# Loading Exp's table behind head 0's two copies, copying head 0's key on ScalarE, and giving the ninth pair of unit 6 the tanh formula

## The chip, the cores and the metric

The kernel runs on one core of a Trainium2 chip. The metric is the device time of one execution in microseconds (us); what is compared is the median of several executions. The core has five engines, each with its own instruction stream: PE (TensorE, matrix products; PEld is its loading of weights), DVE (VectorE), ACT (ScalarE), POOL (GpSimd) and SP (SyncE, which here only issues DMAs). An engine works through its stream in order and waits for the others through semaphores.

## The reference

Two layers follow each other: attention whose mask comes from nearest centroids, and a gated feed-forward layer behind an RMS norm.

```python
def _attn_ref(q, k, v, centroids):            # q, k, v: 4 x 8 x 768 x 64; centroids: 8 x 16 x 64
    scale = 1.0 / np.sqrt(D)
    q_n, k_n, c_n = (a / (norm(a) + 1e-06) for a in (q, k, centroids))
    q_assign = np.argmax(np.einsum('bhsd,hcd->bhsc', q_n, c_n), axis=-1)
    k_assign = np.argmax(np.einsum('bhsd,hcd->bhsc', k_n, c_n), axis=-1)
    mask = q_assign[:, :, :, None] == k_assign[:, :, None, :]
    scores = np.where(mask, scale * (q @ k.T), -1000000000.0)
    attn = softmax(scores)
    return attn @ v

def _moe_ref(x, w_gate, w_val, w_out, rms_g): # x: 3072 x 512, w_gate and w_val: 512 x 1536
    xn = x / np.sqrt(np.mean(x * x) + 1e-06) * rms_g
    g = xn @ w_gate
    silu = g * (1.0 / (1.0 + np.exp(-g)))
    return silu * (xn @ w_val) @ w_out
```

## The kernel before

The 4 batches of 768 tokens are cut into 8 units of 384 tokens (`UNITS`, numbered 0 to 7). For each unit the kernel computes the attention of 8 heads, and while the heads of unit u run, the feed-forward work of unit u-1 and the output products of unit u-2 are woven between them. The 32 pairs of batch and head are in 8 groups of 4. The mask is folded into the score product: the key and query tiles (`kext`, `qext`) hold 64 rows of numbers and 16 rows that say which centroid is nearest, so that one product with 80 rows gives masked scores.

The program order is written out by hand; each engine gets its instructions in that order.

The start is what the first two edits touch. ACT takes the square root for the centroids' norm (L182, `c_norm`), which needs one table of functions, and then an Exp on one column (L184, `first_exp`), whose result nobody reads: it makes the table for Exp come early. Each change of table appears as an ACT_TABLE_LOAD in ACT's stream. DVE scales the centroids (L187, L188), PE transposes them (L192), DVE copies them into `cblk` (L193, L194). For a head, `trans` transposes its key or query on PE into a PSUM tile (L221) and copies it to `qkT` (L225 on DVE, or L227 on ACT by a Copy). The PSUM tiles for this come from one pool of three buffers (`ps_g`), so that a fourth transpose waits until the first has been copied. POOL casts `qkT` to bf16 rows of `kext` and `qext` (L240): K0 and K1 are the two halves of a key, Q0 and Q1 of a query, each an instruction of 64 x 384.

Which centroid is nearest comes from `pair_clusters`: PE multiplies `qkT` with `cblk` (L320), DVE transposes the product (L323), takes the largest of each 16 (L326) and compares (L327, both inputs in SBUF, into a bf16 tile `pads`). `head` puts the result under the key and the query (L332). The hand-written order of POOL's casts at the start is: K0, Q0, K1 of head 0; K0, Q0, K1 of head 1; K0, K1, Q0 of head 2 and of head 3; Q1 of heads 0 and 1; then the cast of head 0's values (`vcast`, L243), the DMAs of the first quarter of the gate and value weights (L204), and the values of head 1. The product of the first probabilities with the values (`pv`, L366) needs head 0's values. On PE it stands ahead of the cluster products of heads 4 and 5, which the second half of DVE's chain at the start works on. Unit 0's attention is followed by its norm (L391, L402, the steps L144 to L153, L410), the transposes to `xnT` (L425) and the first gate products (L442).

The end is what the third edit touches. A feed-forward unit has 12 pairs (FC = 12): a gate product and a value product, four matmuls each (L442), into buffers of `ps_g`. With `CUT = 16`, pairs 0 to 7 of a unit are woven into the attention, and pairs 8 to 11 come behind it; `rest` is what is left of unit 6, the seventh. SiLU is computed in two ways. Where Exp's table stays loaded, it is a Tanh on ACT (L450), and DVE adds 1 and multiplies by the gate product in PSUM (L451), then multiplies by half the value product (L455). Where `last` holds, no Exp follows: ACT takes Silu (L448), which needs another table, and DVE multiplies once with the value product (L453). The first item of `rest` is pair 8's gate; behind it stands the last head's product with the values (`pv`, whose result DVE scales in L371 and L373), then pair 8's value and the other pairs. After pair 9 come the last squares of unit 7's norm (L393) and its root (`root`), then unit 6's output products (L467), unit 7's 12 pairs, and its output products (L467, L478).

Of the kernel before, what the change touches and what calls it, by code (L numbers as in the profile page):

```python
# [14 lines left out]
ACT = mybir.ActivationFunctionType  # L15
# [7 lines left out]
def kernel(  # L23
# [12 lines left out]
    nc = tc.nc  # L36
# [11 lines left out]
    NU = len(UNITS)  # L48
# [5 lines left out]
    CUT = 2 * FC - 8  # L54
# [117 lines left out]
    off = const.tile([P, 1], F32)  # L172
# [8 lines left out]
    c_norm = const.tile([P, 1], F32)  # L181
    nc.scalar.activation(c_norm, c_ss, ACT.Sqrt)  # L182
    first_exp = const.tile([P, 1], F32)
    nc.scalar.activation(first_exp, off, ACT.Exp)  # L184
    c_inv = const.tile([P, 1], F32)
    nc.vector.reciprocal(c_inv, c_norm)
    nc.vector.tensor_scalar_mul(c_n[:, :D], c_in, c_inv)  # L187
# [2 lines left out]
    def centroids_t():  # L190
        c_ps = ps_s.tile([P, P], F32, tag="s", name="c_ps")
        nc.tensor.transpose(c_ps, c_n, ident_f)  # L192
        nc.vector.tensor_copy(cblk[:D, :, :NC], c_ps[:D].rearrange("d (h c) -> d h c", c=NC))  # L193
        nc.vector.tensor_copy(cblk[D:, :, NC:], c_ps[D:].rearrange("d (h c) -> d h c", c=NC))  # L194
# [17 lines left out]
    def trans(g, h, part, on=None):  # L212
        if (g, h // 2) not in qkT:
            qkT[g, h // 2] = qk32.tile([P, 2, 2, UQ], F32, tag="qkT", name="qkT")
        qk = staged[g * HG + h]
        if g * HG + h >= BH:
            nc.vector.transpose(qkT[g, h // 2][:, h % 2, part], qk[:, part].rearrange("p t d -> p (t d)"))
            return
        ps = ps_g.tile([P, UQ], F32, tag="gen", name="tq")
        for i in range(HT):  # L220
            nc.tensor.transpose(ps[:, i * P:(i + 1) * P], qk[:, part, 2 * i:2 * i + 2].rearrange("p t d -> p (t d)"),  # L221
                                ident_f)
        to, by = qkT[g, h // 2][:, h % 2, part], 1.0 / ZS if part and g < BG else 1.0
        if on is nc.vector:
            nc.vector.tensor_scalar_mul(to, ps, by)  # L225
        else:
            nc.scalar.activation(to, ps, ACT.Copy, scale=by)  # L227
# [84 lines left out]
    def pair_clusters(p, heads=(0, 1)):  # L312
        g, h = divmod(2 * p, HG)
        what = [(h + i, m) for i in heads for m in range(2)]
        at = [slot(2 * p + i, m) for i in heads for m in range(2)]
        r = slice(min(at), max(at) + 32)
        pool = ps_g if p else ps_s
        ps = pool.tile([P, UQ], F32, tag="gen" if p else "s", name="sc")
        for a, (hh, m) in sorted(zip(at, what)):
            nc.tensor.matmul(ps[a:a + 32], lhsT=cblk[:, g * HG + hh], rhs=qkT[g, hh // 2][:, hh % 2, m],  # L320
                             start=True, stop=True)
        sct = asg.tile([P, UQ], F32, tag="scT", name="scT", bufs=2)
        nc.vector.transpose(sct[r], ps[r])  # L323
        cl = sct[r].rearrange("p (b e c) -> p b e c", e=2, c=NC)
        mx = small.tile([P, NB, 2], F32, tag="mx", name="mx")[r]
        nc.vector.tensor_reduce(mx, cl, axis=AX, op=ALU.max)  # L326
        nc.vector.tensor_tensor(pads[p][r, :, :NC].rearrange("p b c e -> p b e c"), cl,  # L327
                                mx.unsqueeze(3).broadcast_to([mx.shape[0], NB, 2, NC]), op=ALU.is_equal)
# [105 lines left out]
    def gv(u, f, val):  # L434
        if f == 0 and not val:
            gvT[u] = xp.tile([P, FC, UQ], BF16, tag="gvT", name="gvT")
        w = wv if val else wg
        n = UNITS[u][2] * P
        full = ps_g.tile([P, UQ], F32, tag="gen", name="val" if val else "gate")
        ps = full[:, :n]  # L440
        for c in range(CC):
            nc.tensor.matmul(ps, lhsT=w[:, c, f * P:(f + 1) * P], rhs=xnT[u][:, c, :n], start=c == 0, stop=c == CC - 1)  # L442
        last = u == NU - 1 or (u, f >= CUT // 2) == (NU - 2, True)
        if not val:
            th = gate.tile([P, UQ], F32, tag="th", name="th")[:, :n]
            gates[u] = th
            if last:
                nc.scalar.activation(th, ps, ACT.Silu)  # L448
            else:
                nc.scalar.activation(th, ps, ACT.Tanh, scale=0.5)  # L450
                nc.vector.scalar_tensor_tensor(th, th, 1.0, ps, op0=ALU.add, op1=ALU.mult)  # L451
        elif last:
            nc.vector.tensor_mul(gvT[u][:, f, :n], gates[u], ps)  # L453
        else:
            nc.vector.scalar_tensor_tensor(gvT[u][:, f, :n], gates[u], 0.5, ps, op0=ALU.mult, op1=ALU.mult)  # L455
# [89 lines left out]
    def ffn_work(u):  # L545
        n = UNITS[u][2] / HT
        return [(0.64 * n, lambda f=f, val=val: gv(u, f, val)) for f in range(FC) for val in (False, True)]
# [15 lines left out]

    K0, K1, Q0, Q1 = (1, 0), (1, 1), (0, 0), (0, 1)
    pool_ = nc.gpsimd
    trans(0, 0, 1, nc.vector)
    centroids_t()
    trans(0, 0, 0)
    trans(0, 1, 1)
    pair_clusters(0, (0,))  # L570
    casts(pool_, 0, K0, Q0, K1)
# [173 lines left out]
```

## Time and profile before

| | |
|---|---|
| Device time, median of 4 runs | 327.99 us (327.66 to 328.29) |
| Device time of the profiled execution | 327.66 us |
| Its span, from the first to the last instruction | 325.9 us |
| Instructions | 7780 |
| Granted TensorE clock in the profiled execution | 1.00 |
| DMA traffic | 34.63 MB, mean 106 GB/s |

The span is the part of the device time in which the program's instructions run; 1.8 us lie around it. All times in what follows count from the span's start. In a line of the timeline the columns are: start and length in us, engine, line of the program, operation, tile written and tiles read, size, count, and in brackets the idle time before it and what ended it. Lines with the same group may be merged into one with a count. The end of a matmul is modelled. A line of the windows holds, behind the stretch and its length, the busy time and the number of instructions of each engine, the granted clock, the share of the DMA engines and their rate.

### The profile page before, as it was taken

What the parts mean: (1) busy time and instruction counts of PE and PEld (TensorE: products, weight loads), DVE (VectorE), ACT (ScalarE), POOL (GpSimd) and SP (SyncE); (2) the same over time, 40 slices, a digit from 0 to 9 for tenths busy, and PEclk for the clock granted to TensorE, in tenths of its full rate; (3) what the DMA queues carried; (4) which work ended last, traced back from release to release, by engine and by line L of the source; (5) the groups of instructions that cost most, each with busy time, mean ns of one, the idle gap of its engine ahead of it and who ended that gap; (6) DMA issues with size and microseconds to landing.
All of it is one profiled execution on the core that took longest, in us unless ns stands there. A gap on an engine that the chain in (4) does not pass through costs nothing.

```text
span 325.9 us, 7780 instructions
## 1 busy us (share of the span) xinstructions
PE 318.2 (98%) x2853; PEld 190.5 (58%) x2853; DVE 219.4 (67%) x501; ACT 245.6 (75%) x424; POOL 137.9 (42%) x277
## 2 busy tenths in 40 slices
PE   7999899999999999999999999999999999999996
PEld 3546656655556655665566555665566656654654
DVE  5999977979578676878677785876265645671430
ACT  5899988977769867897778867897779868862322
POOL 6999499998727265441916256350000000000000
DMA  7999995996546644562646440000700040004002
GB/s 252 356 271 246 229 163 101 168 172 152 86 72 155 151 88 72 113 150 70 103 87 133 139 113 34 8 20 1 148 2 0 2 113 34 0 2 132 16 1 97
DMA packets 90310, 34.63 MB, mean 106 GB/s; under 512 B 71968, under 2 KB 87200, under 8 KB 90272
## 3 DMA queue, kind: packets, MB, share of 16 engines
q1 hardware_dynamic: 81104, 27.84, 36.3%
q0 software_dynamic: 8880, 5.91, 11.0%
q8 instruction: 22, 0.36, 0.4%
q10 hardware_dynamic: 288, 0.39, 0.4%
q14 instruction: 16, 0.13, 0.1%
HBM read 28.61 MB, written 6.29 MB: 107 GB/s over the span
## 4 chain that ended last, share of the span: by engine, by line
PE 85%; DVE 9%; ACT 3%; issue 1%; DMA 1%; DVEq 0%; ACTq 0%
PE val L442 18%; PE o L467 18%; PE gate L442 18%; PE s L348 17%; PE acc L366 9%; PE sc L254 3%; DVE kext L332 1%; DVE qext L332 1%; DVE pads L327 1%; DMA boot<-in_centroids_dram 1%; PE o L478 1%; ACT pT L352 1%; DVE qkT L225 1%; DVE xn L391 1%; DVE scT L323 1%
## 5 line engine op out<-in xcount | busy, mean ns | idle before, releaser
L352 ACT ACTIVATE pT<-s,off 128x768 bf16<-128x768 f32 x192 | 170.9, 904 | 30.9 <-PE s L348 30.1
L348 PE MATMUL s<-qext,kext 80*128 80x384 bf16 x384 | 94.8, 328 | 1.6 <-ACT pT L352 0.8
L442 PE MATMUL val<-xnT,wv 128*128 128x384 bf16 x384 | 78.1, 326 | 0.4 <-ACT th L448 0.4
L442 PE MATMUL gate<-xnT,wg 128*128 128x384 bf16 x384 | 78.3, 325 | 0.1
L467 PE MATMUL o<-wo,gvT 128*128 128x512 bf16 x276 | 67.7, 378 | 0.0
L451 DVE SCALAR_TENSOR_TENSOR th<-th,gate 128x384 f32<-128x384 f32 x80 | 44.0, 551 | 33.1 <-ACT th L450 32.5
L348 PEld LDWEIGHTS <-kext 80*128 80x128 bf16 x384 | 36.4, 98 | 35.1 <-issue 7.5
L455 DVE SCALAR_TENSOR_TENSOR gvT<-th,val 128x384 bf16<-128x384 f32 x80 | 44.0, 550 | 9.4 <-PE val L442 3.9
L442 PEld LDWEIGHTS <-wg 128*128 128x128 bf16 x384 | 36.1, 97 | 23.4 <-issue 0.8
L240 POOL CAST qext<-qkT 64x384 bf16<-64x384 f32 x64 | 35.6, 563 | 32.5 <-DVE inv L371 19.2
L366 PEld LDWEIGHTS <-pT 128*128 128x128 bf16 x1152 | 43.4, 97 | 10.1 <-DVE x L373 1.1
L442 PEld LDWEIGHTS <-wv 128*128 128x128 bf16 x384 | 35.7, 97 | 23.2 <-issue 1.3
L450 ACT ACTIVATE th<-gate 128x384 f32<-128x384 f32 x80 | 39.2, 490 | 12.3 <-PE gate L442 11.5
L366 PE MATMUL acc<-vbf,pT 128*128 128x65 bf16 x1152 | 45.7, 193 | 0.6 <-ACT pT L352 0.2
L467 PEld LDWEIGHTS <-gvT 128*128 128x128 bf16 x276 | 26.0, 97 | 26.1 <-issue 0.2
L297 POOL DMA_DIRECT2D qext<-oh x48 | 23.1, 491 | 29.5 <-DVE oh L286 29.5
L240 POOL CAST kext<-qkT 64x384 bf16<-64x384 f32 x58 | 31.4, 541 | 4.3 <-DVE qkT L225 2.4
L470 ACT COPY o_sb<-o 128x512 f32<-128x512 f32 x23 | 13.5, 585 | 17.6 <-PE o L467 17.6
L297 POOL DMA_DIRECT2D kext<-oh x48 | 23.1, 488 | 8.1 <-DVE oh L286 7.8
L371 DVE RECIPROCAL inv<-acc 128x6 f32<-128x6 f32 x32 | 6.0, 188 | 23.9 <-PE acc L366 23.5
L453 DVE TENSOR_TENSOR gvT<-th,val 128x384 bf16<-128x384 f32 x16 | 8.8, 555 | 16.0 <-PE val L442 8.6
L373 DVE TENSOR_TENSOR x<-acc,inv 128x384 f32<-128x384 f32 x32 | 17.8, 558 | 1.1
(79 smaller groups left out, 238.2 us busy)
## 6 DMA issues: line engine op xcount, KB each, us to landing
vs<-in_v_dram SPq DMA_DIRECT2D x32, 192.0 KB, 4.2
out_dram<-o_sb SPq DMA_DIRECT2D x23, 256.0 KB, 2.7
qk<-in_q_dram SPq DMA_DIRECT2D x72, 48.0 KB, 2.8
qk<-in_k_dram SPq DMA_DIRECT2D x72, 48.0 KB, 2.6
qk<-in_q_dram SPq DMA_DIRECT2D x14, 192.0 KB, 4.6
qk<-in_k_dram SPq DMA_DIRECT2D x12, 192.0 KB, 4.8
wg<-in_moe_w_gate_dram POOLq DMA_DIRECT2D x4, 384.0 KB, 9.2
wv<-in_moe_w_val_dram POOLq DMA_DIRECT2D x4, 384.0 KB, 10.5
```

What stands on the lines that cost most here:

```text
L240: on.tensor_copy(to, of)
L297: on.dma_start(out=ext[D:D + NC, h, e * UQ:(e + 1) * UQ], in_=put[g, m][32 * h + e * NC:32 * h + (e + 1) * NC])
L348: nc.tensor.matmul(ps[:, j, :w] if nt == HT else flat[:, j * w:(j + 1) * w], lhsT=cols(kext[g % 4][:KR, hh], g, kc // HT, kc % HT * P, (kc ...
L352: nc.scalar.activation(pT[u, h][:, n * i:n * i + n, :w], of, ACT.Exp, bias=off, scale=scale if g >= BG else scale * ZS)
L366: nc.tensor.matmul(acc[:, h % 2, t], lhsT=pT[u, h][:, kc, t * P:(t + 1) * P], rhs=vbf[g % 4][:, hh, kc % HT * 2 + kc // HT], start=kc == 0 ...
L373: nc.vector.tensor_tensor(dst, acc[:, :, :nt, :D], inv[:, :, :nt].unsqueeze(3).broadcast_to([P, 2, nt, D]), op=ALU.mult)
L442: nc.tensor.matmul(ps, lhsT=w[:, c, f * P:(f + 1) * P], rhs=xnT[u][:, c, :n], start=c == 0, stop=c == CC - 1)
L450: nc.scalar.activation(th, ps, ACT.Tanh, scale=0.5)
L451: nc.vector.scalar_tensor_tensor(th, th, 1.0, ps, op0=ALU.add, op1=ALU.mult)
L455: nc.vector.scalar_tensor_tensor(gvT[u][:, f, :n], gates[u], 0.5, ps, op0=ALU.mult, op1=ALU.mult)
L467: nc.tensor.matmul(outs[u], lhsT=gvT[u][:, f, t * P:(t + 1) * P], rhs=wo[:, f], start=f == 0, stop=f == FC - 1)
L470: nc.scalar.copy(o, outs[u])
```

## The change

Three edits. The Exp on one column is moved from behind the square root to behind head 0's query copy. Head 0's key copy, `trans(0, 0, 1)`, runs on ACT instead of DVE. In the seventh unit (unit 6) the pair 8, the first of the four behind the attention, takes the Tanh formula instead of Silu.

```diff
     first_exp = const.tile([P, 1], F32)
-    nc.scalar.activation(first_exp, off, ACT.Exp)
     c_inv = const.tile([P, 1], F32)
...
-        last = u == NU - 1 or (u, f >= CUT // 2) == (NU - 2, True)
+        last = u == NU - 1 or (u, f > CUT // 2) == (NU - 2, True)
...
     K0, K1, Q0, Q1 = (1, 0), (1, 1), (0, 0), (0, 1)
     pool_ = nc.gpsimd
-    trans(0, 0, 1, nc.vector)
+    trans(0, 0, 1)
     centroids_t()
     trans(0, 0, 0)
+    nc.scalar.activation(first_exp, off, ACT.Exp)
     trans(0, 1, 1)
     pair_clusters(0, (0,))
     casts(pool_, 0, K0, Q0, K1)
```

In the built program ACT's stream at the start is: square root's table, square root, key copy and query copy of head 0, Exp's table, the Exp, then seven more copies. At the end it is: Tanh of pair 8, Silu's table, Silu of pair 9. DVE loses one copy (L225) and gains one L451, which stands ahead of the last head's L371 and L373; pair 8's L453 becomes an L455. PE, POOL and SP keep their instructions and their order.

## The prediction

> **What bounds the kernel now.** The page comes first, then the busy times by stage, then the timeline of the two stages that the change touches.
>
> ```profile
> PE 318.2 (98%) x2853; PEld 190.5 (58%) x2853; DVE 219.4 (67%) x501; ACT 245.6 (75%) x424; POOL 137.9 (42%) x277
> ...
> PE 85%; DVE 9%; ACT 3%; issue 1%; DMA 1%; DVEq 0%; ACTq 0%
> ```
>
> PE is busy for 98% of the span, yet 9% of the chain of waits that ended last is DVE's. The stages say where:
>
> ```profile
> 0.00:24.00 24.00, 21.15 (x172) 11.36 (x173) 19.65 (x44) 18.48 (x31) 20.18 (x43) 1.00 0.97 295
> 24.00:41.00 17.00, 15.57 (x188) 11.10 (x187) 15.87 (x47) 16.50 (x24) 12.48 (x21) 1.00 1.21 236
> 41.00:281.00 240.00, 239.92 (x2213) 143.91 (x2212) 167.43 (x376) 192.19 (x330) 105.28 (x215) 1.00 0.44 90
> 281.00:292.00 11.00, 10.60 (x94) 6.58 (x93) 7.15 (x21) 9.02 (x23) 0.00 (x0) 1.00 0.01 1
> ```
>
> The columns after the stretch are PE, PEld, DVE, ACT, POOL. From 41 to 281 us PE idles 0.08 us of 240, so a delay present at 41 is carried to the end whole. Before 41 the chain runs through DVE: from the clusters' first transpose at 7.16 to the normalized tokens at 40.34 it hardly pauses. Both edits lie outside the PE stage, one at 4 to 8 us and one at 286 us.
>
> **The start, before.**
>
> ```profile
> 4.08 0.20 ACT L182 ACTIVATE c_norm<-c_ss 128x1 f32<-128x1 f32 x1 [1.15 <-DVE c_ss L180]
> 4.31 1.28 ACT L184 ACT_TABLE_LOAD   x1
> 5.60 0.20 ACT L184 ACTIVATE first_exp<-off 128x1 f32<-128x1 f32 x1
> 5.71 0.85 ACT L227 ACTIVATE qkT<-tq 128x384 f32<-128x384 f32 x2
> ```
>
> The load stands where ACT has little else to do: the copy behind it, head 0's query, needs transposes that PE ends at 5.65. So taking the load from before it gains only 5.71 - 5.69 = 0.02 us (a copy starts 0.04 after its transposes, as at 7.60 and 7.64). The clusters' products wait for that copy, and DVE's chain for them. That the key's copy leaves DVE (0.55 us at 4.85) lets the centroids' two copies start about 0.07 earlier, but they were done at 6.02 and the query at 6.18: nothing more.
>
> **What the moved load delays.** Behind query 0 ACT now does the load, 6.17 to 7.46, the small Exp, 7.47 to 7.67, and then head 1's key copy, 7.58 to 8.06 (copies overlap the instruction before by 0.09, as 5.60 + 0.20 and 5.71 show). That copy ran at 6.08 to 6.56. Queued behind it on ACT are the copies of head 1's query (7.96 for 7.64) and head 2, and on PE head 2's query transposes, which need its PSUM buffer (8.11 for 7.76). Its readers are PE's products of head 1 (now 8.5, needed by DVE at 10.4: all of this is hidden) and POOL's cast, which had waited for POOL alone:
>
> ```profile
> 7.58 0.61 POOL L240 CAST kext<-qkT 64x384 bf16<-64x384 f32 x1
> ```
>
> It now starts at 8.06 + 0.06 = 8.12, 0.54 late. POOL then has no free time until head 0's value cast, eleven casts on:
>
> ```profile
> 8.86 0.78 POOL L240 CAST kext<-qkT 64x384 bf16<-64x384 f32 x1
> ...
> 13.70 1.16 POOL L240 CAST qext<-qkT 64x384 bf16<-64x384 f32 x2
> 14.92 0.50 POOL L243 CAST vbf<-vs 128x384 bf16<-128x384 f32 x1
> 15.37 0.90 POOL L204 DMA_DIRECT2D wg<-in_moe_w_gate_dram  x1
> ```
>
> The value cast ends at 15.42 and PE's first value product starts at 15.47, having waited for it. Behind that product PE runs without a pause to the second pair's cluster products, which end at 17.99. DVE takes them at 18.37, when it is free by itself (18.34). With the 0.02 gained and 0.04 to wake DVE, the first 18.37 - 0.02 - 17.99 - 0.04 = 0.32 us of a late value cast cost nothing, and all beyond goes into DVE's chain. A delay of 0.54 would cost 0.2.
>
> **The delay grows.** Five comparisons (L327) in DVE's chain and POOL's casts hold each other up:
>
> ```profile
> 8.35 0.84 DVE L327 TENSOR_TENSOR pads<-scT,mx 64x384 bf16<-64x384 f32 x1
> ...
> 11.70 0.86 DVE L327 TENSOR_TENSOR pads<-scT,mx 64x384 bf16<-64x384 f32 x1
> ...
> 15.01 0.85 DVE L327 TENSOR_TENSOR pads<-scT,mx 128x384 bf16<-128x384 f32 x1
> ...
> 19.57 0.64 DVE L327 TENSOR_TENSOR pads<-scT,mx 128x384 bf16<-128x384 f32 x1
> ...
> 24.72 0.60 DVE L327 TENSOR_TENSOR pads<-scT,mx 128x384 bf16<-128x384 f32 x1
> ```
>
> Free, one takes 0.60. Where POOL is inside a cast (casts end at 8.80, 12.16, 15.42) it ends 0.39 to 0.43 after that cast. A cast that starts during one ends 0.44 to 0.45 after it (9.19 and 9.64; 12.56 and 13.00), with 0.78 to 0.80 instead of 0.61. Thus each meeting lengthens both. The Trainium skill has the reason: its page "SBUF — State Buffer", section "SBUF: two separate sides", says that VectorE with two SBUF inputs and GpSimd take a shared port pair as an exclusive lock, whoever starts first holding it for the whole instruction. By a bandwidth shared in proportion both would slow for the time they overlap; the rows show one waiting instead, and the rule agrees.
>
> Before, the third meeting came late enough to fall on the value cast itself, and cost POOL nothing ahead of it. Walking the same durations with POOL at 8.12: the first comparison (8.32) waits for the cast that ends at 8.73 and ends at 9.12, the next cast at 9.57, and the sixth of the late casts starts at 11.61. The second comparison is ready at 11.63, and 0.02 us can't be called.
> - Cast first: comparison ends 12.62, next cast 13.07; the third comparison (15.07) falls on the last query cast, ends at 16.00, and the value cast at 16.34: 0.92 late. DVE's transpose at 18.37 becomes 18.95: +0.58. At 25.25 the fifth comparison, free before, falls on a key cast and DVE is +0.81.
> - Comparison first: it ends at 12.23, the casts go back, the third meets the cast before, and the value cast ends at 16.65, 1.23 late: +0.89, and +1.12 after the fifth.
>
> Two later DVE lines (L240 at 27.7 with 0.68 against 0.37, L391 at 33.6 with 0.92 against 0.56) pay such waits too and may win or lose 0.3 to 0.4 by where they fall; I take zero, as POOL and DVE are late by about the same there. Bounds for the start: 0.1 (POOL catches up) to 1.5 (1.12 plus 0.36).
>
> The load's own price is 1.28 with 0.01 behind it, at 4.31 behind idle time and at 286.45 behind work alike. The Trainium skill's page "ScalarE: Activation LUTs", section "What ACT_TABLE_LOAD costs", adds a drain of 1.38 to each switch, which speaks against moving it between copies; by that the key copy would be 1.38 later still and the result nearer 330. Neither row here shows a drain.
>
> **The end.**
>
> ```profile
> 286.45 1.28 ACT L448 ACT_TABLE_LOAD   x1
> ...
> 287.74 0.49 ACT L448 ACTIVATE th<-gate 128x384 f32<-128x384 f32 x1
> ```
>
> ```profile
> 287.07 0.81 PE L442 MATMUL gate<-xnT,wg 128*128 128x384 bf16 x4
> 288.29 0.81 PE L442 MATMUL val<-xnT,wv 128*128 128x384 bf16 x4 [0.40 <-ACT th L448]
> ```
>
> PE waits for pair 8's Silu to free its PSUM buffer, and that waits for the table. With Tanh, pair 8's activation runs at 286.30 to 286.80 (0.49, like L450), the load to 288.10, pair 9's Silu at 288.11, about as before (288.13). Added on DVE is one product (L451, 0.55): 286.83 to 287.39, ahead of the last head's reciprocal (0.20) and scaling (0.56), which end at 288.09 instead of 287.41; then pair 8's product, 288.01 to 288.56. PE's buffer for value 9 is free at 287.39, so it starts at 287.73, not 288.29. Gate 10 waits for pair 8's product: 288.56 + 0.05 = 288.61 instead of 288.93. From there on PE is 0.32 ahead: the last Silu ends at 291.26 and the output products start at 291.31 instead of 291.62. The squares behind the scaling run at 288.5 as before, and unit 7's transposed tokens, issued at 294.50 with 3.7 to land, are there at 298.2, before PE asks at 298.9. So -0.32; bounds 0 and -0.56 (value 9's own gain).
>
> **Sum.** Start +0.81 or +1.12, end -0.32: +0.49 or +0.80; I take +0.6. The profiled execution's span of 325.9 becomes 326.5, with 1.8 around it 328.3 from its 327.66. That execution is the fastest of the four shown, 0.33 below the median; against 327.99 it is 328.6. The likeliest case's own range is 328.3 to 329.0. What this kernel can tell from no change is 0.2%, or 0.66 us, so the forecast lies just inside that.
>
> **Rivals.**
> 1. POOL makes the delay good: the comparisons meet fewer casts than I walk, the value cast is late by 0.54 or less, the start costs 0.2 or nothing and the end pays it back. For it: each meeting turns on hundredths. Against: no free time on POOL before 15.42. 327.7 to 328.0. It decides while the value cast is late by less than 0.32 + 0.32 = 0.64.
> 2. The waits add up: comparison first, and one of the lines at 27.7 or 33.6 losing 0.36 more: 327.99 + 1.12 + 0.36 - 0.32 = 329.15, slower. It decides from a value cast over 1.2 late.
> 3. The change doesn't do what it says: a table is loaded before head 0's copies after all. Then only the end counts, 327.7. Against: the copies at 294.41 run under Silu's table with no load of their own.
>
> **Chances.** Forecast 0.60, rival 1 0.24, rival 2 0.12, rival 3 0.04. Slower by over 0.2%: half of the forecast's share and a little more (0.32), and rival 2: 0.44. Faster by over 0.2% needs a gain of 0.66, more than 0.32 + 0.02 unless the later meetings fall well: 0.05. Within: 0.51. The range takes rivals 1 and 2 in: 327.7 to 329.3.
>
> **What would show it.** ACT's load at 6.2 and the next key copy at 7.6; POOL's cast at 8.1; the value cast ending at 16.3 or 16.7, PE's first value product just behind; DVE's transpose at about 19; PE without the 0.40 wait near 288 but with a short one before gate 10. Wrong if the value cast ends before 16.05, or if PE's stretch from 41 on begins less than 0.4 later.

## The result and the profile after

The changed kernel takes 328.39 us in the median of 37 runs (327.73 to 329.84), the kernel before 327.88 in 58 (327.19 to 330.0). The ratio is 1.002 with a 95% interval of 1.0012 to 1.0027, a loss of 0.4 to 0.9 us; the two medians lie 0.51 apart. The profiled execution took 328.76 us, with a span of 327.0.

Its lines are numbered one lower than before between L184 and the moved Exp (L568). First the page's chain that ended last, by engine:

```profile
PE 86%; DVE 7%; POOL 2%; ACT 2%; issue 1%; DMA 1%; DVEq 0%; ACTq 0%; POOLq 0%
```

POOL is in the chain now, and was not before. ACT's timeline at the start, with start and length first:

```profile
4.84 0.49 ACT L226 ACTIVATE qkT<-tq 128x384 f32<-128x384 f32 x1 [0.26 <-PE tq L220]
6.21 0.49 ACT L226 ACTIVATE qkT<-tq 128x384 f32<-128x384 f32 x1 [0.88 <-PE tq L220]
6.72 1.28 ACT L568 ACT_TABLE_LOAD   x1
8.01 0.20 ACT L568 ACTIVATE first_exp<-off 128x1 f32<-128x1 f32 x1
8.12 0.47 ACT L226 ACTIVATE qkT<-tq 128x384 f32<-128x384 f32 x1
```

The two copies, the load, the Exp and head 1's key copy follow each other as built. All of it is 0.5 us later than in the profile before, and so is the clusters' first transpose on DVE, after the change:

```profile
7.68 0.57 DVE L322 STREAM_TRANSPOSE scT<-sc 64x384 f32<-64x384 f32 x1 [1.22 <-PE sc L319]
```

and before it:

```profile
7.16 0.58 DVE L323 STREAM_TRANSPOSE scT<-sc 64x384 f32<-64x384 f32 x1 [1.13 <-PE sc L320]
```

The 0.5 us come from ahead of the moved load: from the end of query 0's transposes on PE to this instruction it is 1.50 us with the change and 1.51 before. With the same start the first experiment below has it at 7.14, and over twelve profiles it lies anywhere from 6.69 to 7.68 (the last section says what differs). So from here on times at the start are given against that transpose, called the anchor.

POOL's timeline of the same stretch:

```profile
8.66 0.62 POOL L239 CAST kext<-qkT 64x384 bf16<-64x384 f32 x1 [0.62 <-ACT qkT L226]
9.20 0.91 POOL L239 CAST qext<-qkT 64x384 bf16<-64x384 f32 x1
...
16.19 0.66 POOL L242 CAST vbf<-vs 128x384 bf16<-128x384 f32 x1
```

POOL now waits 0.62 for the key copy, and the value cast (L242) ends at 16.86, 9.18 after the anchor; before it was 8.26. PE's timeline shows who pays:

```profile
16.91 0.71 PE L365 MATMUL acc<-vbf,pT 128*128 128x65 bf16 x18 [0.96 <-POOL vbf L242]
17.45 0.85 PE L220 MATMUL tq<-ident_f,qk 128*128 128x128 f32 x6
18.14 0.51 PE L347 MATMUL s<-qext,kext 80*128 80x384 bf16 x2
18.57 0.85 PE L319 MATMUL sc<-qkT,cblk 128*32 128x384 f32 x8
```

DVE's comparisons, and the transpose of heads 4 and 5 that waits for the last of these products:

```profile
8.87 0.80 DVE L326 TENSOR_TENSOR pads<-scT,mx 64x384 bf16<-64x384 f32 x1
...
12.17 1.01 DVE L326 TENSOR_TENSOR pads<-scT,mx 64x384 bf16<-64x384 f32 x1
...
15.62 0.89 DVE L326 TENSOR_TENSOR pads<-scT,mx 128x384 bf16<-128x384 f32 x1
...
19.49 0.58 DVE L322 STREAM_TRANSPOSE scT<-sc 128x384 f32<-128x384 f32 x1 [0.50 <-PE sc L319]
...
20.70 0.94 DVE L326 TENSOR_TENSOR pads<-scT,mx 128x384 bf16<-128x384 f32 x1
...
26.14 0.60 DVE L326 TENSOR_TENSOR pads<-scT,mx 128x384 bf16<-128x384 f32 x1
```

Before, the fourth of these lines stood at 18.37, without a wait:

```profile
18.37 0.58 DVE L323 STREAM_TRANSPOSE scT<-sc 128x384 f32<-128x384 f32 x1
```

DVE stood idle 0.50 us for PE, where it had run through. The transpose comes 11.82 after the anchor, for 11.21. Of the 0.61, 0.14 are longer comparisons ahead of it (0.80 + 1.01 + 0.89 for 0.84 + 0.86 + 0.85), the rest the wait. The fourth comparison adds 0.30 (0.94 for 0.64). The sum, +0.90, stands at every later instruction of DVE's chain up to the last transposes of the normalized tokens on PE, after the change:

```profile
41.82 0.40 PE L424 MATMUL tx<-ident,xn 128*128 128x128 bf16 x4 [0.26 <-DVE xn L409]
```

and before it:

```profile
40.39 0.40 PE L425 MATMUL tx<-ident,xn 128*128 128x128 bf16 x4 [0.27 <-DVE xn L410]
```

They end 34.54 after the anchor, for 33.63. Then PE carries it, as the windows say (the columns after the stretch are PE, PEld, DVE, ACT, POOL):

```profile
42.00:282.00 240.00, 239.92 (x2215) 143.91 (x2213) 167.73 (x376) 192.18 (x330) 105.69 (x216) 1.00 0.46 91
```

At the end, PE from gate 9 to gate 10, and DVE around pair 8:

```profile
288.51 0.81 PE L441 MATMUL gate<-xnT,wg 128*128 128x384 bf16 x4
289.16 0.81 PE L441 MATMUL val<-xnT,wv 128*128 128x384 bf16 x4
290.04 0.81 PE L441 MATMUL gate<-xnT,wg 128*128 128x384 bf16 x4
```

```profile
288.28 0.55 DVE L450 SCALAR_TENSOR_TENSOR th<-th,gate 128x384 f32<-128x384 f32 x1 [0.46 <-ACT th L449]
288.75 0.19 DVE L370 RECIPROCAL inv<-acc 128x6 f32<-128x6 f32 x1
288.97 0.56 DVE L372 TENSOR_TENSOR x<-acc,inv 128x384 f32<-128x384 f32 x1
289.44 0.54 DVE L454 SCALAR_TENSOR_TENSOR gvT<-th,val 128x384 bf16<-128x384 f32 x1
```

Value 9 follows gate 9 at once, 0.65 us behind it; gate 10 waits for pair 8's product, which ends at 289.98. From pair 8's gate to unit 6's first output product it is 6.07 us instead of 6.395: 0.325 won. The two instructions, after the change:

```profile
286.66 0.81 PE L441 MATMUL gate<-xnT,wg 128*128 128x384 bf16 x4
...
292.73 2.54 PE L466 MATMUL o<-wo,gvT 128*128 128x512 bf16 x11
```

and before it:

```profile
285.23 0.81 PE L442 MATMUL gate<-xnT,wg 128*128 128x384 bf16 x4
...
291.62 1.67 PE L467 MATMUL o<-wo,gvT 128*128 128x512 bf16 x7
```

### The profile page after: what moved, and what is told of

It reads as the page before. It is cut to its first block, busy times and chain, and to the rows that moved or that the text cites. A ratio compares the mean times of both kernels' runs of the same rounds, so it can differ in the third digit from the quotient of the medians.

```text
span 327.0 us, 7779 instructions
## 1 busy us (share of the span) xinstructions
PE 319.2 (98%) x2853; PEld 190.9 (58%) x2853; DVE 219.8 (67%) x501; ACT 246.0 (75%) x425; POOL 138.3 (42%) x277
## 4 chain that ended last, share of the span: by engine, by line
PE 86%; DVE 7%; POOL 2%; ACT 2%; issue 1%; DMA 1%; DVEq 0%; ACTq 0%; POOLq 0%
PE gate L441 18%; PE o L466 18%; PE val L441 18%; PE s L347 17%; PE acc L365 10%; PE sc L253 3%; POOL kext L239 1%; POOL qext L239 1%; DMA boot<-in_centroids_dram 1%; DVE x L372 1%; PE o L477 1%; ACT pT L351 1%; DVE qkT L224 1%; DVE xn L390 1%; DVE xn L409 1%
## 5 line engine op out<-in xcount | busy, mean ns | idle before, releaser
L216 DVE STREAM_TRANSPOSE qkT<-qk 128x384 f32<-128x384 f32 x36 | 18.1, 550 | 0.1
```

## The experiments

The theory: the load makes head 1's key copy late, with it POOL's casts, with them the value cast, PE's products behind it and DVE's chain; DVE and POOL lengthen each other on the way; the Tanh pair gives 0.32 back. Against it stood that the loss is ACT's own, that it is the late anchor of the one profile, that the key's change of engine makes it, and that the Tanh pair costs.

In the table, "anchor to heads 4, 5" is the time from the anchor to DVE's transpose of these heads, "to norm" to the end of PE's last transposes of the normalized tokens, and "end" from pair 8's gate to unit 6's outputs, each from the run's profile. "Sum" adds the differences of the last two columns from before. "Measured" is the ratio less one times the time of before, with its interval.

| run | anchor to heads 4, 5 | to norm | end | sum | measured |
|---|---|---|---|---|---|
| before | 11.21 | 33.63 | 6.395 | | |
| changed | 11.82 | 34.54 | 6.070 | +0.59 | +0.66 (+0.39 to +0.89) |
| start edits only | 11.82 | 34.55 | 6.394 | +0.92 | +0.72 (+0.43 to +1.05) |
| Tanh pair only | 11.21 | 33.62 | 6.070 | -0.34 | -0.36 (-0.66 to -0.07) |
| load moved only | 11.74 | 34.37 | 6.398 | +0.74 | +0.59 (+0.29 to +0.88) |
| extra POOL cast | 11.83 | 34.46 | 6.398 | +0.83 | +0.82 (+0.46 to +1.18) |
| changed, values early | 11.91 | 34.58 | 6.070 | +0.63 | +0.39 (+0.07 to +0.72) |
| before, Tanh, values early | 11.06 | 33.54 | 6.072 | -0.41 | -0.52 (-0.85 to -0.16) |
| before, values early | 11.07 | 33.55 | 6.398 | -0.08 | -0.29 (-0.62 to +0.03) |
| changed, both early | 11.19 | 34.06 | 6.077 | +0.11 | 0.00 (-0.26 to +0.29) |
| changed, queries early | 11.82 | 34.55 | 6.077 | +0.60 | +0.46 (+0.16 to +0.72) |
| before, Tanh, both early | 11.50 | 33.87 | 6.077 | -0.08 | -0.07 (-0.33 to +0.20) |

In each run the sum lies inside the measured interval, which is about 0.3 us to either side; on average the sums lie 0.10 above the measured values. To that accuracy these two stretches hold what the edits move.

**The start edits alone.** The last edit of the change is left out.

```diff
-        last = u == NU - 1 or (u, f > CUT // 2) == (NU - 2, True)
+        last = u == NU - 1 or (u, f >= CUT // 2) == (NU - 2, True)
```

> Exp's load behind head 0's copies and head 0's key copy on ACT; pair 8 keeps Silu. Theory (POOL's casts late, value cast late by 0.9 us, DVE's chain with it): 0.8 to 1.0 us slower than before, ratio 1.0025 to 1.003, and the value cast ends 0.9 us later against the clusters' first transpose than before. Rival (the 0.52 us by which the changed kernel's profile is late at the first cluster products is the change's own, and POOL's part adds to it): 1.3 to 1.5 us slower. Rival (no loss at the start, the changed kernel is slow for its last edit): no change.

0.4 to 1.05 us slower, the value cast 9.18 after the anchor for 8.26, and the anchor at 7.14. The loss is the start's, and it doesn't need the late anchor: the anchor was back at the old place, and the loss stayed.

**The Tanh pair alone,** on the kernel before:

```diff
-        last = u == NU - 1 or (u, f >= CUT // 2) == (NU - 2, True)
+        last = u == NU - 1 or (u, f > CUT // 2) == (NU - 2, True)
```

> Pair 8 by Tanh alone. Theory: PE's 0.40 us wait for value 9 goes, a shorter one comes ahead of gate 10, and PE's output products of unit 6 start 0.32 us earlier against pair 8's gate: 0.3 us faster than before, ratio 0.999. Rival (the added product on DVE costs what the table's wait gave): no change, and a wait of 0.4 us or more ahead of gate 10.

0.1 to 0.7 us faster, and PE's stretch from pair 8's gate is shorter by 0.325. The wait ahead of gate 10 is 0.23 (288.23 - 287.35 - 0.65):

```profile
287.35 0.81 PE L442 MATMUL val<-xnT,wv 128*128 128x384 bf16 x4
288.23 0.81 PE L442 MATMUL gate<-xnT,wg 128*128 128x384 bf16 x4
```

**The load moved alone,** head 0's key copy on DVE:

```diff
-    trans(0, 0, 1)
+    trans(0, 0, 1, nc.vector)
     centroids_t()
     trans(0, 0, 0)
     nc.scalar.activation(first_exp, off, ACT.Exp)
```

> Exp's load behind head 0's query copy as in the change, but head 0's key copy stays on DVE and pair 8 keeps Silu. Theory (who copies head 0's key makes no difference; head 1's key copy behind the load does): as with both start edits, 0.8 to 1.0 us slower than before. Rival (the key copy on ACT is part of the loss): 0.4 us or less slower.

0.3 to 0.9 slower; the value cast at 9.10. Measured and sum lie a little below the 0.8 expected, but the load alone makes most of the loss. The 0.18 between the two sums comes from where comparisons met casts (the five took 0.73, 1.00, 0.89, 0.59 and 0.85, against 0.80, 1.00, 0.89, 0.94 and 0.59); the two measured intervals overlap.

**An extra POOL cast** in the kernel before. Head 0's K1 is cast twice, with the same result.

```diff
-    casts(pool_, 0, K0, Q0, K1)
+    casts(pool_, 0, K0, Q0, K1, K1)
```

> The kernel before, with one of head 0's casts (K1) done twice on POOL, ahead of head 1's first; no table load is moved and ACT's stream is untouched. POOL is 0.67 us late from head 1's first cast on, where the change makes it 0.54 late. Theory (the loss comes through POOL alone): 0.5 to 1.2 us slower, with the value cast 0.7 to 1.3 late and DVE's transpose of heads 4 and 5 waiting for PE. Rival (the loss is ACT's own: the load ahead of the copies): no change, POOL's lateness being hidden.

0.5 to 1.2 slower, with Exp's load where it always was (4.27). DVE's timeline has the same 0.50 wait as the changed kernel's:

```profile
19.48 0.58 DVE L323 STREAM_TRANSPOSE scT<-sc 128x384 f32<-128x384 f32 x1 [0.50 <-PE sc L320]
```

So POOL's lateness, without any of ACT's, is enough for a loss of this size. The rival, that the loss is ACT's own, falls.

**The value cast ahead of two others,** in the changed kernel:

```diff
+    vcast(0)
     casts(pool_, 0, Q1)
     casts(pool_, 1, Q1)
-    vcast(0)
```

> The changed kernel with head 0's value cast put ahead of the two Q1 casts on POOL, so that it ends 1.24 us earlier, and those two 0.51 later. Theory (the start's loss of 0.9 us runs from the value cast over PE into DVE's chain): PE's first value product no longer waits for POOL at the end of its stretch, DVE's transpose of heads 4 and 5 is again DVE's own (about 0.1 to 0.2 us later than before against the clusters' first transpose), and the kernel is 0.1 to 0.4 us faster than before, 0.5 to 0.9 faster than the changed one. Rival (DVE and POOL hold each other up so that the loss comes whatever the value cast does): as the changed kernel, 0.4 to 0.7 slower than before.

The theory failed here: 0.1 to 0.7 slower than before, and DVE's transpose at 11.91, no earlier than in the changed kernel. The value cast ended 7.70 after the anchor and PE's first value product no longer waited for it, but ACT's timeline has another wait for POOL:

```profile
16.48 0.49 ACT L226 ACTIVATE qkT<-tq 128x384 f32<-128x384 f32 x1 [1.67 <-POOL qext L239]
```

This is the copy of head 6's key, the third head of group 1. (Two of the expectations below call it group 1's first key; that one, head 4's, stands earlier and waits for no buffer.) There are three `qkT` buffers, each for two heads, and head 6's key takes the one of heads 0 and 1, whose last reader is POOL's second Q1 cast. Behind it on ACT stand head 1's exponentials, whose end PE needs ahead of the same cluster products. So POOL's lateness has a second way out. The changed kernel's profile has this wait too, but shorter:

```profile
16.16 0.49 ACT L226 ACTIVATE qkT<-tq 128x384 f32<-128x384 f32 x1 [0.92 <-POOL qext L239]
```

There it costs DVE's chain nothing, by an estimate from these rows. In this run it is 2.68 us from the copy's start to DVE's transpose (16.48 to 19.16). In the changed kernel that would put the transpose at 16.16 + 2.68 = 18.84, ahead of 19.02, when DVE is free by itself (the transposes ahead of this one end at 18.99). What made the wait count here is the new order: behind the value cast, the second Q1 cast ends 9.20 after the anchor, for 8.45 in the changed kernel. The run put one wait in the place of another.

**The same order in the kernel before,** with the Tanh pair and without:

> The kernel before with the Tanh pair and with the value cast ahead of the two Q1 casts. Theory: the value cast was not on the path of the kernel before (0.3 us of slack), so only the Tanh pair counts, 0.3 to 0.4 us faster than before, up to 0.3 either way for where the comparisons fall. Rival (ACT's copy of group 1's first key, which waits for the later Q1 cast's buffer, takes the place): 0 to 0.5 slower than before.

> The kernel before with the value cast ahead of the two Q1 casts, nothing else. Theory: no change within 0.3 us, DVE's chain being the bound and the value cast having slack. Rival (the value cast holds the kernel before too): 0.3 us or more faster.

With the Tanh pair 0.2 to 0.85 faster than before, 327.26 us against 327.70: the lowest median of the study, though its interval overlaps that of the Tanh pair alone. Without the Tanh pair -0.29, with an interval that takes in zero. In both, the third comparison met a query cast that ended sooner than the value cast had, and took 0.72 for 0.85.

**Both ways opened** in the changed kernel: head 3's three casts go behind the Q1 casts and the value cast.

```diff
-    casts(pool_, 3, K0, K1, Q0)
     trans(1, 0, 1)
     casts(pool_, 0, Q1)
     casts(pool_, 1, Q1)
     vcast(0)
+    casts(pool_, 3, K0, K1, Q0)
```

> The changed kernel with POOL's three casts of head 3 (needed last) put behind the two Q1 casts and the value cast, so that both of POOL's ways out of its lateness come 1.85 us earlier: the value cast (PE's first value product waits for it) and the second Q1 cast (ACT's copy of group 1's first key waits for its buffer). Theory: with both open the loss of the start goes; DVE's transpose of heads 4 and 5 comes 11.2 to 11.4 us after the clusters' first (11.82 in the changed kernel), the norm's last transpose at 33.6 to 33.9 (34.54), and the kernel is 0 to 0.4 us faster than before. Rival (DVE and POOL hold each other up whatever waits on POOL): 34.4 or more, slower than before by 0.4 to 0.7.

DVE's transpose is back at 11.19, with no wait:

```profile
18.43 0.58 DVE L322 STREAM_TRANSPOSE scT<-sc 128x384 f32<-128x384 f32 x1
```

Of the 0.63 regained, 0.47 is the wait; the rest is nearly all the third comparison, 0.75 for 0.89. The time is the kernel before's, 1.0 (0.9992 to 1.0009), at the edge of what was expected, because the norm is still 0.43 late. DVE's timeline of this run says where:

```profile
33.28 0.92 DVE L390 SCALAR_TENSOR_TENSOR xn<-x 128x384 bf16<-128x384 f32 x1
...
34.13 0.90 DVE L390 SCALAR_TENSOR_TENSOR xn<-x 128x384 bf16<-128x384 f32 x1
```

and in the kernel before:

```profile
33.11 0.55 DVE L391 SCALAR_TENSOR_TENSOR xn<-x 128x384 bf16<-128x384 f32 x1
...
33.59 0.91 DVE L391 SCALAR_TENSOR_TENSOR xn<-x 128x384 bf16<-128x384 f32 x1
```

The first of the two squares now meets the value cast of head 7 (POOL, 33.26 to 33.79), as the second meets the next cast in both kernels. That cast comes 26.02 after the anchor, for 25.49 in the kernel before: POOL's lateness was carried this far and paid here.

**Only ACT's way opened:** head 3's casts between the Q1 casts and the value cast.

```diff
     casts(pool_, 1, Q1)
+    casts(pool_, 3, K0, K1, Q0)
     vcast(0)
```

> The changed kernel with head 3's casts behind the two Q1 casts but ahead of the value cast: only ACT's way is opened, the value cast stays where it was. Theory (the two ways are parallel, each enough for the loss): as the changed kernel, transpose of heads 4 and 5 at 11.7 to 11.9, 0.4 to 0.7 us slower than before. Rival (only ACT's wait for the Q1 cast makes the loss): 11.2 to 11.4, not slower than before.

As the changed kernel, 0.2 to 0.7 slower. ACT's copy of head 6's key no longer waits, but PE waits for the value cast, and DVE for PE:

```profile
16.82 0.71 PE L365 MATMUL acc<-vbf,pT 128*128 128x65 bf16 x18 [1.00 <-POOL vbf L242]
```

```profile
19.41 0.58 DVE L322 STREAM_TRANSPOSE scT<-sc 128x384 f32<-128x384 f32 x1 [0.50 <-PE sc L319]
```

This run and the one ahead of it differ only in where the value cast stands, behind or ahead of head 3's casts, and DVE's transpose comes at 11.82 or at 11.19. So the late value cast makes the changed kernel's wait, and ACT's copy is not needed for it. That ACT's way would be enough at the changed kernel's own lateness, as the theory has it, isn't shown: it counted only where the Q1 casts came later still.

**The Tanh pair with both ways opened,** on the kernel before:

> The kernel before with the Tanh pair and with head 3's casts behind the Q1 casts and the value cast. Theory: 0.32 us for the Tanh pair and 0 to 0.2 for a third comparison that meets no cast: 0.3 to 0.6 us faster than before. Rival (head 3's casts, now 1.75 us later, hold its scores): 0 to 0.5 slower than before.

No difference from before, against an expectation of 0.3 to 0.6. With the new order of casts the second and third comparison take 0.99 and 1.02 (0.86 and 0.85 before), and the norm is 0.24 late, most of the Tanh pair's 0.32.

## Why the prediction was right

The forecast, a loss of about 0.6 us at the edge of 0.2%, is what was measured (0.66, from 0.39 to 0.89), and its steps can be read off one by one against the anchor.

- *The load's old place was free, and moving it gains next to nothing.* From the end of query 0's transposes to the anchor it is 1.51 us before and 1.50 with the change.
- *Head 1's first cast 0.54 late.* Against the anchor it starts at 0.98 for 0.42, 0.56 late.
- *The second comparison and a cast within 0.02 us of each other.* They came within 0.02 (12.16 and 12.17 in the changed kernel), the cast first, in every run with the moved load. That is the first of the two walks.
- *The value cast 0.92 late, DVE's transpose +0.58.* 0.92 and 0.61.
- *+0.81 after the fifth comparison.* Here the term was misplaced: the fifth stayed free (0.60, the cast ahead of it ends 0.007 before it starts), and the fourth paid, with 0.30, where I had let it pass and had 0.23 on the fifth. It came to +0.90 in all for the +0.81 of that walk, and that the two are so near is in part luck: in the changed kernel a value cast starts 0.002 us ahead of the fourth comparison. With the load moved alone, and with the extra cast, the comparison came first by about 0.01; the fourth was free and the fifth paid, with 0.85 for 0.60.
- *The lines at 27.7 and 33.6 at zero.* Zero in the changed kernel; 0.43 in the run with both ways opened. The bound was right to be kept.
- *The end, -0.32, with a short wait ahead of gate 10.* -0.325, and a wait of 0.23.
- *The span, 326.5.* It was 327.0; the 0.5 are the profiled execution's own late anchor.

One step was incomplete. The prediction named what is queued behind head 1's key copy on ACT and PE and called it hidden, and held the value cast for the only way from POOL to DVE's chain. For the changed kernel that is what its last two experiments show, 11.82 with the value cast late and 11.19 with it early. But it missed ACT's copy of head 6's key, which waits for a buffer that POOL's second Q1 cast frees and would come next. This changed no number, since that way is shorter (18.84 by the estimate above, for 19.49); but the fix that follows from the prediction, the value cast moved ahead, put the Q1 casts behind it and did not work because of it.

That DVE and POOL wait for each other is borne out by the comparisons' lengths in twelve profiles. Free, one takes 0.58 to 0.60, also where a cast ends within the first 0.08 us of it; where a cast ran on longer, it ends 0.38 to 0.44 after the cast (once 0.54), and a cast that starts during one ends 0.43 to 0.46 after it (a value cast 0.34). This is what the Trainium skill's page "SBUF — State Buffer", section "SBUF: two separate sides", calls an exclusive lock. Which of the operands takes the port was not tried.

The drain of 1.38 us that the Trainium skill's page "ScalarE: Activation LUTs" adds to a table load, in "What ACT_TABLE_LOAD costs", doesn't show: between two copies the load begins 0.02 after the first, takes 1.28, and the Exp starts 0.01 behind it. The measurement decides.

## What to carry to other kernels

The table load cost nothing where its engine waited anyway; behind the first copies it stood ahead of a third copy, whose reader POOL had no slack, and 0.56 us there became 0.9 at the end of the chain. Before moving work onto a queue, list every reader of what comes behind it, and who waits for the buffers that those readers free. Where two engines hold each other up, as DVE and POOL do here, a shift of a tenth moves which instructions meet, so that gains of 0.3 us must be read against an anchor inside the profile, not from spans.

## What the runs showed of the hardware

The first 7 us are not the same from one execution to the next. PE's first transpose took 0.27 us in three profiles and 0.40 to 0.42 in nine (the next one starts 0.11 us after it in those three, 0.21 in the nine), with a granted clock of 1.00 (0.999 in two) in all; the centroids' transpose took 0.33 in six and 0.47 to 0.48 in six. The centroids' DMA was used by DVE from 3.10 to 3.86. Together this moves the anchor by up to 1 us, more than the whole effect studied here, and kernels with the load early (6.69 to 7.65) and late (7.14 to 7.68) have both.

They don't have both equally often: the slow centroids' transpose stands in five of the six profiles with the load late and in one of the six with it early, and the anchor's mean is 7.43 and 7.09. Twelve profiles can't say whether the load's place has a part in that. A delay of 0.34 us in most executions would make the measured differences larger than the table's sums, which start at the anchor; for the six kernels with the load late they are 0.13 smaller on average. So the many runs show no such delay.
